# A GELU-gated MLP beside a 2-D spectral filter: head order by tiles, and two chunks transposed by DMA

## Chip, core and metric

The kernel runs on one core of a Trainium2 chip. The metric is the device time of one execution in microseconds (us), as the median of several runs.

## What is computed

```python
x = A_x                                   # (1, 2048, 512) bf16
xn = layernorm(x)                         # over the last axis, eps 1e-5, no scale or shift
X = rfft2(xn) * (w_r + 1j * w_i)          # over both axes; weights (2048, 257)
y = irfft2(X, s=(2048, 512))              # as bf16
g = xn @ w_gate                           # (512, 1792)
u = xn @ w_up
m = (gelu_tanh(g) * u) @ w_down           # (1792, 512)
out = x + y + m
```

## The kernel before

The 2048 rows are 16 tiles of 128 rows. Four tiles are a chunk (`m` or `b`, 0 to 3). All five engines' programs are written out by hand: `_Prog.op` puts an instruction into its engine's list in the order of the calls, and works out from the names of what it reads and writes which semaphores it must wait for. Each engine runs its own list in order.

**Layer norm and transposes.** Per tile VectorE takes statistics (`ln_stat`, L394), aggregates them (`ln_aggr`, L398, L401), GpSimd raises the variance to -1/2 (`rstd`, L402), and VectorE normalizes into `xn`, four slots of `slots` (`ln_norm`, L406). `trans` (L416) transposes 128x128 blocks on TensorE into PSUM, two of the four column blocks (`dcs`) at a time, eight transposes in a call; VectorE (L426) or ScalarE (ACT, L428) copies the result into `xnT`, fp16, 128 columns of `d` on the partitions. In `xnT` a chunk is a range of 512 columns in each of the four `d` blocks.

**The MLP.** For each chunk, 14 blocks `fc` of 128 hidden columns: `gate` (L699, four matmuls over `d`, then Gelu on ACT, L702, into one of three `gl` buffers) and `up` (L714, four matmuls, then on VectorE the product of PSUM and `gl` into `hT`, L720). The down projection of a pair of tiles is done with seven matrix products (`prod`, L805, seven matmuls each) and sums of blocks (`ssum`, L796; `sum_T`, L764), interleaved with the gates and ups of the next chunk.

**The spectral part.** `butter` (L438 to L442) makes sums and differences of the four `d` blocks of `xnT`; it writes into `fold`, a part of `arena`. `unit_D` (L456 to L459) transforms along `d`, one tile a call; `unit_A` (L489) along part of the rows, two tiles a call; its result goes through DRAM, `scr<-slots`, and comes back as `tv<-scr` (`load_tv`), both on SyncE's DMA queue. `unit_Z` and `unit_B` read all of `tv`. `unit_G`, `unit_M`, `unit_B` and `unit_C` apply the filter (with `Wr`, `Wi`, `cm`), then a second trip through DRAM into `arena`, and `unit_E`, `unit_F` and the final sums.

**Order.** The gates and ups are the backbone. After each, `hook` runs the calls that `at(h, ...)` has put at that number; hooks are counted through the whole kernel (28 for chunk 0; 42 for a later chunk, since products count too). So D, A, butterflies, norms and late loads stand at fixed places between gates and ups. `load_late` issues a load on GpSimd's queue (POOL) after the matmuls that precede it. The first loads are issued by SyncE (SP) and ACT at the start, in program order. `take` picks a PSUM bank out of eight from a rough account of when each comes free.

Lines of the head that the change touches, of the kernel before:

```python
for b, eng in ((0, "sp"), (1, "act")):
    load_x(0, 2, b, eng)
    load_x(2, 2, b, eng)
dma("sp", ident[:], c_id.ap(), w=["ident"])
load_w(wg_sb, wgv, "wg", 0, 3, "act")
load_w(wu_sb, wuv, "wu", 0, 3, "sp")
```

Of the kernel before, what the change touches and what calls it, by code (L numbers as in the profile page):

```python
# [18 lines left out]
P = 128  # L19
NJ = 16  # L20
NFC = 14
LN_EPS = 1e-5
# [105 lines left out]
class _Prog:  # L128


    def __init__(self, nc, es):
        self.nc, self.es = nc, es
        self.q = {e: [] for e in ("pe", "act", "dve", "pool", "sp")}
        self.sem = {}
        self.cnt = {}
        self.known = {e: {} for e in self.q}
        self.lastclk = {e: {} for e in self.q}
        self.clk = {}
        self.writer = {}
        self.readers = {}  # L140
        for e in ("pe", "act", "dve", "pool"):
            self.sem[e] = es.enter_context(nc.semaphore("s_" + e))
            self.cnt[e] = 0
        self.dsem = []

    def op(self, eng, fn, r=(), w=(), dma=False, after=(), own=False):
# [4 lines left out]
        for k in w:  # L151
            if k in self.writer:
                deps.append((self.writer[k], False))
            for ev in self.readers.get(k, ()):
                deps.append((ev, False))
        need = {}
        for (st, val), raw in deps:
            if st == eng and not dma and (eng == "pe" or not (raw or own)):
# [22 lines left out]
        else:  # L181
# [3 lines left out]
            for a, b in known.items():  # L185
                if clk.get(a, 0) < b:
                    clk[a] = b
        clk[ev[0]] = ev[1]
# [22 lines left out]
def bass_parallel_sum__spectral_gfnet__glu_gated_geglu__prompt_kernel(  # L211
# [26 lines left out]
    with ExitStack() as es:  # L238
# [24 lines left out]
        arena = sb("arena", [P, 9216], F16)  # L263
        am = arena[:, 0:4096].rearrange("p (j r c) -> p j r c", j=NJ, r=2)
        fold = [arena[:, 4096 + 2048 * i:6144 + 2048 * i].rearrange("p (a c) -> p a c", a=4) for i in range(2)]
        ev1 = arena[:, 8192:9216].rearrange("p (a c) -> p a c", a=2)
# [20 lines left out]
        hz = xnT[:, 3, 256:512].bitcast(F32).rearrange("p (a b c d) -> p a b c d", a=2, b=2, c=16)  # L287
# [35 lines left out]
        pt = [0.0]  # L323
        act_t = [0.0]
        free = [0.0] * 8

        full = [False] * 8

        def take(n, dur, hold=None, need=False, fills=True):

            ok = [i for i in range(9 - n) if not need or all(full[i:i + n])]
            i = min(ok, key=lambda i: max(free[i:i + n]))
            for k in range(i, i + n):
                full[k] = fills
            pt[0] += dur
            if hold is None:
                act_t[0] = max(act_t[0], pt[0] + 0.25) + 0.62
                end = act_t[0]
            else:
                end = pt[0] + hold  # L340
            for k in range(i, i + n):
                free[k] = end
            return i

# [14 lines left out]
        op("dve", lambda e: e.memset(dumm[:], 0.0), w=[("sl", 12)])  # L359
        op("pool", lambda e: e.memset(mhalf[:], -0.5), w=["mhalf"])  # L360
        for b, eng in ((0, "sp"), (1, "act")):
            load_x(0, 2, b, eng)
            load_x(2, 2, b, eng)
        dma("sp", ident[:], c_id.ap(), w=["ident"])
        load_w(wg_sb, wgv, "wg", 0, 3, "act")
        load_w(wu_sb, wuv, "wu", 0, 3, "sp")
        load_w(wg_sb, wgv, "wg", 3, 6, "act")
        op("act", lambda e: e.activation(warm_o[:], mhalf[:, 0:1], ACT.Gelu_apprx_tanh), r=["mhalf"], w=["warm_o"])
        load_w(wu_sb, wuv, "wu", 3, 6, "sp")
        load_x(4, 4, 0, "sp")  # L370
        load_x(4, 4, 1, "sp")
        dma("sp", fd[:], c_fd.ap(), w=["fd"])
        dma("sp", am, c_am.ap().rearrange("p (j r c) -> p j r c", j=NJ, r=2), w=["am"])
        load_w(wg_sb, wgv, "wg", 6, 10, "sp")
        load_w(wu_sb, wuv, "wu", 6, 10, "sp")
        load_x(8, 4, 0, "sp")
        load_x(8, 4, 1, "sp")
        load_w(wg_sb, wgv, "wg", 10, 14, "sp")
        load_w(wu_sb, wuv, "wu", 10, 14, "sp")
# [4 lines left out]
        def warm(n):  # L384
# [5 lines left out]
            op("pe", f, r=[("sl", 12)], w=[("ps", 7)])  # L390
# [5 lines left out]
        def ln_aggr(j0, n):  # L396
            for j in range(j0, j0 + n):
                op("dve", lambda e, j=j: e.bn_aggr(ag[:, j, :], st[:, j, :]), r=[("st", j)], w=[("ag", j)])  # L398
            sl = slice(j0, j0 + n)
            js = range(j0, j0 + n)  # L400
            op("dve", lambda e: e.tensor_scalar(vpe[:, sl], ag[:, sl, 1], LN_EPS, None, ALU.add), r=[("ag", j) for j in js], w=[("vpe", j) for j in js])  # L401
            op("pool", lambda e: e.tensor_tensor(rstd[:, sl], vpe[:, sl], mhalf[:, 0:n], ALU.pow), r=[("vpe", j) for j in js] + ["mhalf"],  # L402
               w=[("rstd", j) for j in js])

        def ln_norm(j):
            op("dve", lambda e: e.tensor_scalar(xn[:, j % 4, :], x_sb[:, j, :], ag[:, j, 0:1], rstd[:, j:j + 1], ALU.subtract, ALU.mult),  # L406
               r=[("x", j, 0), ("x", j, 1), ("ag", j), ("rstd", j)], w=[("sl", 8 + j % 4)])

        def trans(m, dcs, jjs, eng="dve"):
            bk = take(1, 0.45, 1.2, fills=False)  # L410
# [9 lines left out]
            c0 = m * 512 + jjs[0] * P  # L420
            n = len(dcs)
            dst = xnT[:, dcs[0]:dcs[0] + n, c0:c0 + w]
            src = bank_h(bk)[:, 0:n * w].rearrange("p (a c) -> p a c", a=n)
            ks = [("xnT", m, dc, jj) for dc in dcs for jj in jjs]
            if eng == "dve":
                op("dve", lambda e: e.tensor_copy(dst, src), r=[("ps", bk)], w=ks)  # L426
            else:
                op("act", lambda e: e.activation(dst, src, ACT.Copy), r=[("ps", bk)], w=ks)  # L428
# [4 lines left out]
        def butter(m, part):  # L433
            f = fold[m % 2]
            k = ("fold", m % 2)
            sl = slice(m * 512, (m + 1) * 512)
            if part == 0:
                op("dve", lambda e: e.tensor_tensor(ev1, xnT[:, 0:2, sl], xnT[:, 2:4, sl], ALU.add), r=xk(m), w=["ev1"])  # L438
                op("dve", lambda e: e.tensor_tensor(f[:, 2:4, :], xnT[:, 0:2, sl], xnT[:, 2:4, sl], ALU.subtract), r=xk(m), w=[k + (2,), k + (3,)])
            else:  # L440
                op("dve", lambda e: e.tensor_tensor(f[:, 0, :], ev1[:, 0, :], ev1[:, 1, :], ALU.add), r=["ev1"], w=[k + (0,)])
                op("dve", lambda e: e.tensor_tensor(f[:, 1, :], ev1[:, 0, :], ev1[:, 1, :], ALU.subtract), r=["ev1"], w=[k + (1,)])  # L442

# [3 lines left out]
        def unit_D(j):  # L447
# [15 lines left out]
            op("act", lambda e: e.activation(x4[:].rearrange("p (a c r) -> p a c r", a=2, r=4),  # L463
# [15 lines left out]
        def unit_A(h):  # L479
# [17 lines left out]
            op("act", lambda e: e.activation(t4, pair(bk), ACT.Copy, scale=SC_A), r=[("ps", bk), ("ps", bk + 1)], w=tk)  # L497
# [3 lines left out]
            if h % 2:  # L501
                load_tv(h // 2)
# [599 lines left out]
```

## Time and profile before

| What | Value |
|---|---|
| Median of 3 runs (lowest to highest) | 185.04 us (184.81 to 186.04) |
| Profiled execution, its own time | 183.82 us |
| Span of its profile | 182.0 us |
| TensorE (PE) busy | 173.6 us, 95% |
| Weight loads (PEld) | 108.1 us, 59% |
| VectorE (DVE) | 134.7 us, 74% |
| ScalarE (ACT) | 98.2 us, 54% |
| GpSimd (POOL) | 27.3 us, 15% |
| DMA moved | 25.14 MB, 138 GB/s over the span |

The profile is of one execution. It gives the busy time of each engine, the span in 40 slices (4.55 us each), who waited for whom, the chain of work that ended last, and for each DMA issue the time until its data landed. A line such as L699 is a line of the kernel before. TensorE's matmuls are pipelined and their ends are modelled, so the distance from start to start of two groups says more than the duration of one.

### The profile page before, as it was taken

The page shows a single profiled execution, that of the slowest core. Times are in us where ns is not written, and L with a number is a line of the kernel's source. Part 1 is how long each engine was busy: PE and PEld are TensorE (multiplying, and loading weights), DVE is VectorE, ACT ScalarE, POOL GpSimd, SP SyncE. Part 2 cuts the span into 40 slices and gives each one's busy share as a digit, 9 for nine tenths or more (in the row PEclk, how much of TensorE's full clock was granted, in tenths as well). Part 3 has the DMA queues.
Part 4 walks back from the last instruction along what each step waited for, and adds up shares of the span by engine and source line. Part 5 has one row for each costly group of instructions (what it writes and reads, how often), then busy time and mean ns, then how long its engine had stood idle before and what let it go on. Part 6 is the DMA issues. An engine that isn't in the chain of part 4 may idle for free.

```text
span 182.0 us, 3627 instructions
## 1 busy us (share of the span) xinstructions
PE 173.6 (95%) x1413; PEld 108.1 (59%) x1413; DVE 134.7 (74%) x297; ACT 98.2 (54%) x168; POOL 27.3 (15%) x52
## 2 busy tenths in 40 slices
PE   7499998999999999999999999999999999999992
PEld 2285464655555666755466646664577757776881
DVE  1859899898996428359886688465745989788993
ACT  3144537466486633234776557654486667766530
POOL 0200513528444400540100000000000000000000
PEclk9999999999999999999999999999999999999999
DMA  4999997987899872341232224444102211312004
GB/s 128 322 294 368 263 271 250 255 210 165 224 205 296 238 242 61 109 146 39 86 115 79 89 66 119 115 115 119 58 0 60 59 33 32 86 29 59 4 0 115
DMA packets 18785, 25.14 MB, mean 138 GB/s; under 512 B 2128, under 2 KB 15312, under 8 KB 18384
## 3 DMA queue, kind: packets, MB, share of 16 engines
q1 hardware_dynamic: 14848, 16.29, 33.0%
q0 software_dynamic: 2464, 7.38, 14.4%
q10 hardware_dynamic: 1456, 1.25, 2.4%
q8 instruction: 11, 0.18, 0.4%
q14 instruction: 6, 0.05, 0.1%
HBM read 18.61 MB, written 6.29 MB: 137 GB/s over the span
## 4 chain that ended last, share of the span: by engine, by line
PE 76%; DVE 17%; issue 2%; DMA 2%; POOL 1%; ACT 1%; DVEq 0%
PE ps L699 23%; PE ps L714 23%; PE ps L805 18%; DVE small L394 3%; DVE hT L796 3%; PE ps L603 2%; DVE hT L720 2%; PE ps L629 2%; DMA x_sb<-in_A_x_dram 2%; PE ps L667 2%; PE ps L489 2%; PE ps L416 2%; DVE slots L406 1%; POOL rstd L402 1%; PE ps L574 1%
## 5 line engine op out<-in xcount | busy, mean ns | idle before, releaser
L699 PE MATMUL ps<-xnT,wg 128*128 128x512 f16 (+1 forms) x236 | 58.1, 368 | 0.8 <-ACT xnT L428 0.8
L714 PE MATMUL ps<-xnT,wu 128*128 128x512 f16 (+1 forms) x236 | 58.1, 368 | 0.1
L702 ACT ACTIVATE gl<-ps 128x512 bf16<-128x512 f32 (+1 forms) x59 | 34.0, 576 | 41.4 <-PE ps L699 41.0
L720 DVE TENSOR_TENSOR hT<-ps,gl 128x512 bf16<-128x512 f32 (+1 forms) x59 | 38.6, 658 | 18.5 <-PE ps L714 17.8
L699 PEld LDWEIGHTS ps<-xnT,wg 128*128 128x128 bf16 x236 | 22.2, 98 | 19.8 <-issue 1.5
L714 PEld LDWEIGHTS ps<-xnT,wu 128*128 128x128 bf16 x236 | 22.2, 98 | 18.1 <-issue 1.0
L805 PE MATMUL ps<-wd,hT 128*128 128x256 bf16 (+1 forms) x224 | 29.4, 273 | 0.0
L805 PEld LDWEIGHTS ps<-wd,hT 128*128 128x128 bf16 x224 | 21.4, 98 | 7.0 <-DVE hT L796 0.4
L810 ACT ACTIVATE ps<-ps 128x256 f32<-128x256 f32 x32 | 11.8, 369 | 12.2 <-PE ps L805 11.9
L394 DVE BATCH_NORM_STATS2 small<-x_sb 128x6 f32<-128x512 bf16 x16 | 10.8, 682 | 3.1 <-DMA x_sb<-in_A_x_dram 3.0
L463 ACT ACTIVATE slots<-ps 128x512 f16<-128x512 f32 x16 | 9.6, 597 | 5.6 <-PE ps L459 5.5
L585 DVE TENSOR_TENSOR slots<-slots,Wr 128x1024 bf16<-128x1024 f16 x8 | 5.5, 693 | 8.4 <-ACT slots L580 8.2
L611 ACT ACTIVATE slots<-ps 128x1024 bf16<-128x1024 f32 x8 | 8.2, 1024 | 4.4 <-PE ps L603 3.4
L351 POOL DMA_DIRECT2D Wr<-in_A_w_r_dram x16 | 8.0, 498 | 16.8 <-PE ps L714 13.6
L636 ACT ACTIVATE slots<-ps 128x512 bf16<-128x512 f32 x16 | 9.6, 598 | 1.4 <-PE ps L629 1.3
L805 PE MATMUL ps<-xnT,hT 128*128 128x256 f16 x70 | 9.3, 273 | 0.0
L351 POOL DMA_DIRECT2D Wi<-in_A_w_i_dram x16 | 7.9, 497 | 8.1 <-PE ps L714 4.0
L497 ACT ACTIVATE slots<-ps 128x1024 f16<-128x1024 f32 x8 | 7.9, 1022 | 1.8 <-PE ps L489 1.6
L796 DVE TENSOR_TENSOR hT<-hT 128x896 bf16<-128x896 bf16 x14 | 8.5, 620 | 0.2
L673 ACT ACTIVATE slots<-ps 128x1024 bf16<-128x1024 f32 x8 | 8.2, 1022 | 0.7 <-PE ps L667 0.3
L402 POOL TENSOR_TENSOR rstd<-vpe,mhalf 128x4 f32<-128x4 f32 (+1 forms) x5 | 4.6, 920 | 24.0 <-DVE vpe L401 24.0
L580 ACT ACTIVATE slots<-ps 128x1024 f16<-128x1024 f32 x8 | 8.2, 1020 | 0.0
(93 smaller groups left out, 207.2 us busy)
## 6 DMA issues: line engine op xcount, KB each, us to landing
Wr<-in_A_w_r_dram POOLq DMA_DIRECT2D x16, 128.5 KB, 4.6
Wi<-in_A_w_i_dram POOLq DMA_DIRECT2D x16, 128.5 KB, 3.7
scr<-slots SPq DMA_DIRECT2D x16, 128.0 KB, 4.1
tv<-scr SPq DMA_DIRECT2D x8, 256.0 KB, 4.1
scr<-slots SPq DMA_DIRECT2D x8, 256.0 KB, 2.3
arena<-scr SPq DMA_DIRECT2D x8, 256.0 KB, 3.5
x_sb<-in_A_x_dram SPq DMA_DIRECT2D x6, 256.0 KB, 12.0
out_dram<-x_sb SPq DMA_DIRECT2D x10, 128.0 KB, 2.4
```

The lines of the kernel that those rows point to most:

```text
L351: op("pool", lambda e: e.dma_start(dst, src), w=keys, dma=True, after=[("pe", pr.cnt["pe"])])
L394: op("dve", lambda e: e.bn_stats(st[:, j, :], x_sb[:, j, :]), r=[("x", j, 0), ("x", j, 1)], w=[("st", j)])
L463: op("act", lambda e: e.activation(x4[:].rearrange("p (a c r) -> p a c r", a=2, r=4), bank(bk).rearrange("p (a r c) -> p a c r", a=2, r=4) ...
L580: op("act", lambda e: e.activation(xc[s2], pair(bk), ACT.Copy, scale=SC_B), r=[("ps", bk), ("ps", bk + 1)], w=ck)
L636: op("act", lambda e: e.activation(z[:], bank(bk).rearrange("p (a c) -> p a c", a=4), ACT.Copy, scale=SC_E), r=[("ps", bk)], w=[zk])
L699: ins = e.matmul(bank(bg)[:, 0:n], wg_sb[:, dc, fc * P:(fc + 1) * P], xnT[:, dc, c0:c0 + n], start=(dc == 0), stop=(dc == 3))
L702: op("act", lambda e: e.activation(gl[k % 3][:, 0:n], bank(bg)[:, 0:n], ACT.Gelu_apprx_tanh), r=[("ps", bg)], w=[("gl", k % 3)])
L714: ins = e.matmul(bank(bu)[:, 0:n], wu_sb[:, dc, fc * P:(fc + 1) * P], xnT[:, dc, c0:c0 + n], start=(dc == 0), stop=(dc == 3))
L720: op("dve", lambda e: e.tensor_tensor(hT[b % 2][:, fc, h0:h0 + n], bank(bu)[:, 0:n], gl[k % 3][:, 0:n], ALU.mult), r=[("ps", bu), ("gl", k ...
L796: op("dve", lambda e: e.tensor_tensor(Ss[i][0], a, c, o), r=ak + ck + (Ss[2][1] if i == 3 else []), w=Ss[i][1])
L805: ins = e.matmul(o, L[:, fc, :], R[fc], start=(start and fc == 0), stop=(fc == 6), skip_group_check=True)
L810: op("act", lambda e: e.activation(half(y, k), half(x, i), ACT.Copy), w=bkey(x, y), own=True)
```

## The change

- *Loads.* The first two tiles of x are loaded one by one (half on SyncE, half on ACT); all weights are loaded from SyncE's queue; x of chunk 1 comes in two parts between the weights; `fd` and `am` come after it; x of chunks 2 and 3 comes last.
- *Head.* Statistics, norm, transposes and copies of tiles 0 and 1 are done tile by tile. The gates of blocks 0 to 2 are then computed for tile 0 and after that for tile 1 (`gates_by_tile`). Six blocks (`NH`) instead of three are first computed for tiles 0 and 1 only, and for tiles 2 and 3 after them.
- *Chunks 2 and 3.* Each is transposed by one DMA from `slots` into `xnT` on SyncE's queue (`trans_dma`), in a layout where the four `d` blocks of a tile stand side by side; `xd` gives the view of a chunk in either layout, and `gate`, `up` and `butter` read through it. Chunks 0 and 1 stay on TensorE (`MT`).
- *Butterfly.* The first sums go to `fold` itself and one extra row (`evx`); the last addition is in place.
- *Hooks.* Norms, transposes, butterflies, D, A, `load_tv`, `sum_T` and the late loads stand at other hooks.
- *Banks.* `_Prog` keeps an estimated time for each engine and event (`c=` gives an instruction's), and `take` picks a bank by when its last user is expected to finish. The wait of the second `up` product (`wait=True`) is dropped; `gl` is addressed by block and tile.

```diff
+NH = 6
+MT = 2
+TVH = (5, 5, 5, 4)
...
+        def xd(m):
+            if m < MT:
+                return xnT[:, m, :].rearrange("p (d j t) -> p d j t", d=4, j=4)
+            return xnT[:, m, :].rearrange("p (j d t) -> p d j t", d=4, j=4)
...
-        for b, eng in ((0, "sp"), (1, "act")):
-            load_x(0, 2, b, eng)
-            load_x(2, 2, b, eng)
-        dma("sp", ident[:], c_id.ap(), w=["ident"])
-        load_w(wg_sb, wgv, "wg", 0, 3, "act")
+        for j in range(2):
+            for b, eng in ((0, "sp"), (1, "act")):
+                load_x(j, 1, b, eng)
+        dma("act", ident[:], c_id.ap(), w=["ident"])
+        load_w(wg_sb, wgv, "wg", 0, 3, "sp")
+        load_x(2, 2, 0, "sp")
+        load_x(2, 2, 1, "sp")
         load_w(wu_sb, wuv, "wu", 0, 3, "sp")
-        load_w(wg_sb, wgv, "wg", 3, 6, "act")
+        load_w(wg_sb, wgv, "wg", 3, 6, "sp")
...
         load_w(wu_sb, wuv, "wu", 3, 6, "sp")
-        load_x(4, 4, 0, "sp")
-        load_x(4, 4, 1, "sp")
+        load_x(4, 2, 0, "sp")
+        load_x(4, 2, 1, "sp")
+        load_w(wg_sb, wgv, "wg", 6, 10, "sp")
+        load_w(wu_sb, wuv, "wu", 6, 10, "sp")
+        load_x(6, 2, 0, "sp")
+        load_x(6, 2, 1, "sp")
         dma("sp", fd[:], c_fd.ap(), w=["fd"])
         dma("sp", am, c_am.ap().rearrange("p (j r c) -> p j r c", j=NJ, r=2), w=["am"])
-        load_w(wg_sb, wgv, "wg", 6, 10, "sp")
-        load_w(wu_sb, wuv, "wu", 6, 10, "sp")
+        load_w(wg_sb, wgv, "wg", 10, 14, "sp")
+        load_w(wu_sb, wuv, "wu", 10, 14, "sp")
         load_x(8, 4, 0, "sp")
         load_x(8, 4, 1, "sp")
-        load_w(wg_sb, wgv, "wg", 10, 14, "sp")
-        load_w(wu_sb, wuv, "wu", 10, 14, "sp")
         load_x(12, 4, 0, "sp")
         load_x(12, 4, 1, "sp")
...
+        def trans_dma(m):
+            op("sp", lambda e: e.dma_start_transpose(xnT[:, m, :].rearrange("p (a c) -> p a c", a=16), slots[:, 8:12, :].rearrange("p a c -> p (a c)")),
+               r=[("sl", 8 + jj) for jj in range(4)], w=[("xnT", m, dc, jj) for dc in range(4) for jj in range(4)], dma=True)
...
             else:
-                op("dve", lambda e: e.tensor_tensor(f[:, 0, :], ev1[:, 0, :], ev1[:, 1, :], ALU.add), r=["ev1"], w=[k + (0,)])
-                op("dve", lambda e: e.tensor_tensor(f[:, 1, :], ev1[:, 0, :], ev1[:, 1, :], ALU.subtract), r=["ev1"], w=[k + (1,)])
+                op("dve", c=0.34, fn=lambda e: e.tensor_tensor(f[:, 1, :], f[:, 0, :], evx, ALU.subtract), r=["evx", k + (0,)], w=[k + (1,)])
+                op("dve", c=0.45, fn=lambda e: e.tensor_tensor(f[:, 0, :], f[:, 0, :], evx, ALU.add), r=["evx"], w=[k + (0,)], own=True)
...
-        for u0, h0 in ((0, 20), (12, 28), (4, 36), (8, 57)):
+        for u0, h0 in ((0, 24), (12, 33), (4, 56), (8, 64)):
...
-        for m in range(1, 4):
-            a = 9 * (m - 1) + 3
-            t = a + 9 + (m == 1)
...
-        for j in range(NJ):
-            h = (9, 11, 13, 15, 18, 20, 22, 23, 26, 28, 30, 32, 35, 36, 37, 38)[j]
-            at(h, (unit_D, j))
-            if j % 4 == 3:
-                at(h + 2, (unit_A, j // 2 - 1), (unit_A, j // 2))
-        at(29, (sum_T, 1))
-        at(31, (sum_T, 2))
-        at(34, (sum_T, 3))
-        at(35, (sum_T, 4))
+        for m, (sh, nh, t, te, f, dh, ah) in enumerate((
+                ((), (), 0, (), (12, 13), (17, 18, 19, 20), (22, 22)),
+                ((2, 3, 8, 10), (13, 14), 17, ("dve", "dve"), (20, 21), (24, 25, 26, 27), (29, 29)),
+                ((22, 23, 24, 25), (27, 28), 28, ("dve", "dve"), (34, 35), (38, 39, 40, 41), (43, 43)),
+                ((32, 33, 36, 37), (39, 40), 40, ("act", "act"), (46, 47), (50, 51, 52, 53), (55, 55)))):
+            for i, h in enumerate(sh):
+                at(h, (ln_stat, 4 * m + i))
+                at(nh[i // 2], (ln_norm, 4 * m + i))
+            if m:
+                at(sh[3], (ln_aggr, 4 * m, 4))
+                if m < MT:
+                    at(t, (trans, m, (0, 1), (0, 1, 2, 3), te[0]))
+                    at(t + 1, (trans, m, (2, 3), (0, 1, 2, 3), te[1]))
+                else:
+                    at(t, (trans_dma, m))
+            for part, h in enumerate(f):
+                at(h, (butter, m, part))
+            for i, h in enumerate(dh):
+                at(h, (unit_D, 4 * m + i))
+            for i, h in enumerate(ah):
+                at(h, (unit_A, 2 * m + i))
+            at(ah[1] + TVH[m], (load_tv, m))
+        for i, h in ((1, 30), (2, 32), (3, 37), (4, 42)):
+            at(h, (sum_T, i))
...
-        warm(14)
+        warm(12)
         ln_stat(0)
+        ln_aggr(0, 1)
         ln_stat(1)
-        ln_aggr(0, 2)
-        ln_stat(2)
+        ln_aggr(1, 1)
         ln_norm(0)
         ln_norm(1)
+        for jj in range(2):
+            trans(0, (0, 1), (jj,), "dve")
+            trans(0, (2, 3), (jj,), "act")
+        ln_stat(2)
         ln_stat(3)
...
+        gates_by_tile((0, 1, 2))
+        up(0, 0, (0, 1))
         ln_norm(2)
         ln_norm(3)
...
+        up(0, 1, (0, 1))
+        up(0, 2, (0, 1))
+        gate(0, 3, (0, 1))
+        gate(0, 4, (0, 1))
         trans(0, (0, 1), (2, 3), "dve")
         trans(0, (2, 3), (2, 3), "act")
+        gate(0, 5, (0, 1))
...
-                jjs = (2, 3) if b == 0 and fc < 3 else (0, 1, 2, 3)
+                jjs = (2, 3) if b == 0 and fc < NH else (0, 1, 2, 3)
+                if b == 0 and fc == 3:
+                    for f2 in range(3, NH):
+                        up(0, f2, (0, 1))
```

## The prediction

> **What bounds the kernel now.** I read the slices of the span first, then who waited for whom on TensorE, the chain that ended last, the groups by shape, the DMA issues and the queue of SyncE in order of time.
>
> ```profile
> PE   7499998999999999999999999999999999999992
> DVE  1859899898996428359886688465745989788993
> PEclk9999999999999999999999999999999999999999
> ```
>
> TensorE is full from the third slice to the last, at the full granted clock, so time can only come from its first 31 us, from its list of work, or from the tail. VectorE is nearly full in slices 3 to 12.
>
> ```profile
> PE ps L416 <- DVE slots L406: 2.3, 2, 1.6
> PE ps L699 <- ACT xnT L428: 0.8, 1, 0.8
> PE ps L456 <- DVE arena L442: 0.6, 1, 0.6
> ```
>
> These are all of TensorE's waits between 7 and 36 us (total, times, longest): 1.6 before the first transpose and 0.8 before the first gate, then 0.7 before chunk 1's transpose at 23.1 (norms late) and 0.6 before chunk 1's first D at 30.8 (butterfly late). After 30.8 starts follow each other without a gap until about 170.
>
> ```profile
> 0.74 3.33 DMA x_sb<-in_A_x_dram
> 4.09 1.29 DVE small L394 x2
> 5.38 0.23 DVE small L398 x2
> 5.63 0.18 DVE vpe L401
> 5.89 0.74 POOL rstd L402
> 6.65 0.75 DVE slots L406 x2
> 7.53 0.62 PE ps L416 x8
> 8.17 0.61 ACT xnT L428
> 8.91 0.60 PE ps L699 x4
> ```
>
> This is the start of the chain (start, us, what): two tiles together, step after step, until the first gate at 8.91. The steady prices come from the same view: eight transposes 0.45, a half-width gate or up 0.44, a full one 0.86, a product 0.765, an A pair 0.98, a D 0.34.
>
> **The change, part by part.**
>
> *Head.* x tiles come one by one and each is normalized and transposed alone. A first half tile is 64 KB. The trace has no such load: 64 KB stores land in 2.0 us, the quickest 128 KB load took 2.8. I take 2.6 (bounds 2.0, and 3.3 as now), so tile 0 is there at 3.3. Statistics 0.68, aggregate 0.15, epsilon 0.18 and steps between: 4.4. The same for tile 1: 5.3. GpSimd's first rstd (0.74) is done by 5.2, the second by 6.1. Norm 0 runs at 5.3, norm 1 at 6.15 to 6.5, and behind it on VectorE the copy of tile 0's transposes (0.42 for twice the columns, so some 0.28). First gate at 6.9 instead of 8.91: **-2.0** (bounds -2.5, -1.2). The two warm-up matmuls removed lie before that; ACT's queue now carries the identity (4.2 us to land now; needed at 5.7). Cover that must hold: the first gate weights are third on SyncE's queue. Ahead of them and with them are 0.69 MB, with tiles 2 and 3 0.95 MB; the slices' rates (128, then 322 GB/s) move that by 5.7, so they land about 6.2, 0.7 before use. Later weights are covered: six blocks on half the columns push block 6 from 14.7 or so (block 3 full now) to 18.7, and its weights are within the first 3.4 MB, there by 14. Chunk 2's x, now behind all weights, is within 6.5 MB of SyncE's loads plus 1 to 1.8 MB of w_down, 27 to 29 us; its statistics come at 31.
>
> *Two waits.* The 0.7 and 0.6 go, since chunk 1's norms and butterfly now sit three or more hooks ahead of use on a less loaded VectorE. I count a new 0.3 where tiles 2 and 3 are copied before their first gate: **-1.0** (bounds -1.3, 0).
>
> *Chunks 2 and 3.* Four groups of eight transposes leave TensorE's full stretch: 4 x 0.45 = **-1.8**, no bound needed. Four copies (0.60 apart) leave VectorE, where TensorE hides them.
>
> *Half blocks.* Three more blocks split: 6 x (2 x 0.44 - 0.86) = **+0.15**. The tile-major layout reads 128-column runs in matmuls and butterflies; shapes stay, and I price this at nothing (no row shows such runs; 1% on the 56 gates and ups of chunks 2 and 3 would be 0.5, on either side).
>
> *Other edits at nothing.* Banks by finish times: TensorE waits on no bank now, and a bad choice would show as a new wait on ACT or VectorE. The butterfly's add in place waits for the subtraction before it, 0.1 or so on VectorE, which TensorE hides except at D. Wr, Wi and cm loads on GpSimd's queue move to later hooks; the last Wi load, at hook 71, has eight hooks (6.5 us) before unit_G reads it, and such loads land in 3.7 to 4.6. The tv loads keep their place in SyncE's order, but for the transposes between them.
>
> Sum so far: -4.65. Adding up the work in the new order gives the same: first D of chunk 2 on TensorE near 47.6, A of chunk 3 at 65.3, Z at 76.5 instead of 81.2.
>
> *The new waits.* Chunks 2 and 3 now wait for one 512 KB DMA each on SyncE, and the butterfly that needs it sits on VectorE, in order: behind it are the products hT of gate and up, behind those the three gl buffers and PSUM banks, and so TensorE.
>
> ```profile
> scr<-slots SPq DMA_DIRECT2D x16, 128.0 KB, 4.1
> tv<-scr SPq DMA_DIRECT2D x8, 256.0 KB, 4.1
> wg<-in_B_w_gate_dram SPq DMA_DIRECT2D x2, 512.0 KB, 11.4
> wd<-in_B_w_down_dram POOLq DMA_DIRECT2D x2, 512.0 KB, 9.8
> ```
>
> No transposing DMA is in this trace (columns: count, size, us to landing). Low end 3.3, the quickest tv load of half the bytes; high end 11.4, the same bytes in a full queue. I take 5.1: the tv load, same queue and same stretch, plus 256 KB more at some 250 GB/s (1.0). It is nearer to tv, because the queues of 35 to 60 us are not the head's.
> The Trainium skill speaks against the change: "VectorE: DVE Perf Modes", The three transpose paths and Rules for kernel authors, lists 390 ns for a 128x128 transpose on TensorE, 1309 by DMA, and advises TensorE where PSUM will do. Sixteen in a row by that figure would be 21 us a chunk (an estimate), and the kernel some 25 us slower. Against it stands 56 ns a transpose in the row above. "DMA: Bandwidth & Descriptors", Latency and other measured facts, gives 261 GB/s for a strided DMA transpose, by which the data alone is 2.0 us (an estimate) and the sum mine.
>
> ```profile
> 29.91 2.66 SPq L347 DMA_DIRECT2D scr<-slots  x4
> 35.95 1.37 SPq L347 DMA_DIRECT2D tv<-scr  x2
> ```
>
> Chunk 2: SyncE reaches the transpose only past the stores and tv loads of chunk 0. Now A starts at 28.2, the second tv load issues at 36.8, 8.6 later. A will start at 30.4, so the transpose issues at 39.6; the norms are done at 38.9. VectorE, by its order (statistics, products, sum_T 1 and 2 at 1.0, norms 1.5 for four, all from the rows), reaches the butterfly at 45.0. Room 5.4: **0**, and 1 us for each us beyond. Chunk 3: norms end at 54.0. From there two sums (0.54), sum_T 4 (1.05) and two products (0.6) come first, and D for chunk 3 is on TensorE at 59.9 with 1.9 of butterfly ahead. Room 4.0: **+1.1**. How long the transpose holds SyncE I don't know: 0.6 like other issues, or all 5; behind it are only scr stores and tv loads of chunks 1 and 2, whose reader is Z, 25 us on.
>
> Chunk 3's spectral path loses its cover. Its A starts at 57.8 now and Z reads tv at 81.2: 23.4 us. In the new order only the A (0.98), six products, six gates or ups and the small G work lie between: 11.0 us. The way through is eviction (first one ends 1.7 after A starts), four stores at 0.66, landing 2.4 to 4.8, tv landing 3.3 to 4.5: 10 to 13.1 us (now all batches take 13.1 or more, with fuller DMA queues). I take 11.5: **+0.5** (bounds 0, 2.1).
>
> Total -4.65 + 1.6 = -3.05. The profiled execution took 183.82 for a span of 182.0, 1.2 under the median 185.04; so 180.8 for one like it, and **182.0** on the median's scale.
>
> **Rivals.**
> 1. *The transposes are hidden.* They land in 4 us or less and the tv path takes 11: 185.04 - 4.65 = 180.4. For it: 3.3 to 3.8 for tv loads at 59 to 67 us. Against: DMA engines 0.8 to 1.0 busy from 30 to 60.
> 2. *The gain turns into waits.* Landing near 6.8: stalls 1.4 + 2.8 + 0.5 cancel 4.65: 185.1. For it: tv loads issued at 45 us took 6.5 to 8.0. Against: those ran beside a full run of Wr and Wi loads, which now leave the stretch of chunk 3's transpose.
> 3. *Slower.* The transposing DMA itself is slow, in place at both butterflies. The price is 2L - 9.4 for a landing L over 5.4; L = 10 gives 10.6, and 185.04 - 4.65 + 0.5 + 10.6 = 191.5. It decides from L = 6.8 on, and is over 1% slower from 7.7. For it: 9.8 and 11.4 for 512 KB. Against: these were queued behind megabytes.
> 4. *The head does less*: x lands at 4.1 as before, first gate at 7.7: 182.8. On the forecast's side of no change.
>
> **How the numbers follow.** A measurement of this kernel tells about 1% from no change: under 183.2 is faster, over 186.9 slower. Forecast with rival 4 (180.8 to 183.2) 0.48, rival 1 0.20, rival 2 0.16, rival 3 0.16. So faster 0.68, same 0.16, slower 0.16. The forecast's own range is 180.2 to 183.6; 179.5 to 186.7 leaves out rival 3 and little below.
>
> **What would show it.** First gate near 6.9, no wait over 0.4 on TensorE from 12 to 45; no transposes of chunks 2 and 3 there; a DMA xnT<-slots twice, about 5 us to landing; VectorE's butterfly (arena<-xnT) for chunk 3 waiting about 1 us for it and TensorE's D behind; Z near 78, waiting for tv 0.5 or so. Wrong: a landing over 7 us, a first gate after 8, or new gaps between 12 and 36 us because weights or x come late.

## The result, and the profile after

The changed kernel took 190.44 us (median of 4 runs, 189.56 to 191.24), the kernel before beside it 185.54; the ratio is 1.0285, 95% interval 1.0218 to 1.0351. The forecast was 182.0 (179.5 to 186.7). The profiled execution took 189.97 for a span of 188.0; before, 183.82 for 182.0. Here and below a median is over all executions of a kernel, and a ratio leaves out those more than 1.5% above its fastest. Lines below are of the changed kernel: D is L482, the butterfly L464 to L469, Z L539, A L515, gate L740, up L754, the DMA transpose L452.

The slices of the span (4.7 us each):

```profile
PE   7699999999499999969999999999999999999992
DVE  3748978777698755337597678637555789887993
PEclk9999999999969999996999999999999999999999
```

TensorE now has two holes, in slices 11 and 18, and in the granted clock the slice behind each has a dip. Who waited for whom on TensorE (total, times, longest):

```profile
PE ps L482 <- DVE arena L469: 2.6, 1, 2.6
PE ps L539 <- DMA tv<-scr: 2.1, 1, 2.1
PE ps L410 <- DVE slots L377: 1.2, 1, 1.2
PE ps L754 <- DMA wu<-in_B_w_up_dram: 0.9, 1, 0.9
PE ps L438 <- DVE slots L428: 0.7, 2, 0.4
PE ps L740 <- ACT xnT L449: 0.3, 1, 0.3
PE ps L598 <- DVE hT L759: 0.3, 1, 0.3
```

The waits of before at chunk 1's transpose and D are gone. New are D of chunk 2 (2.6), Z (2.1) and the first up (0.9). The chain that ended last shows what stands behind them (start, us, what), here its stretch around chunk 2's transpose:

```profile
37.54 2.36 DMA tv<-scr
39.89 8.73 DMA xnT<-slots
...
51.39 0.23 PE ps L482
...
53.79 1.71 PE ps L740 x4
```

The transpose is issued at 39.89 (forecast 39.6) but lands 8.73 later, at 48.6, where the forecast had 5.1. VectorE stood 2.1 for it, TensorE 2.6 (VectorE's waits for both transposes: total, times, longest):

```profile
DVE arena L464 <- DMA xnT<-slots: 2.7, 2, 2.1
```

The gate at 53.79 then takes 1.71, twice its 0.86, since the clock is down. The windows of 1 us show it (window, PE, PEld, DVE, ACT, POOL busy, granted clock, DMA share, GB/s):

```profile
52.00:53.00 1.00, 1.00 (x5) 0.30 (x4) 1.00 (x2) 0.53 (x1) 0.00 (x0) 0.61 0.90 273
53.00:54.00 1.00, 1.00 (x6) 0.62 (x5) 0.97 (x7) 0.17 (x1) 0.30 (x1) 0.50 0.01 0
54.00:55.00 1.00, 1.00 (x4) 0.44 (x3) 1.00 (x2) 0.43 (x1) 1.00 (x1) 0.50 0.74 262
55.00:56.00 1.00, 1.00 (x7) 0.58 (x6) 1.00 (x3) 0.47 (x1) 1.00 (x2) 0.68 0.07 16
```

Four windows give up 0.39 + 0.50 + 0.50 + 0.32 = 1.7 us of full clock. Chunk 3's transpose, issued at 57.6, lands in 5.4; VectorE stands 0.5 for it, TensorE not at all. The second hole is the trip of chunk 3's A through DRAM, in the same chain:

```profile
75.02 3.97 DMA scr<-slots
...
79.05 5.78 DMA tv<-scr
...
84.96 0.22 PE ps L539 x4
...
86.33 1.54 PE ps L754 x4
```

A starts at 71.33 and tv's last load lands at 84.83, 13.5 later (forecast 11.5); Z waits 2.1, and another dip of the clock follows. Meanwhile GpSimd's queue, in order of time:

```profile
42.15 0.49 POOL L369 DMA_DIRECT2D Wi<-in_A_w_i_dram  x1 [1.46 <-PE ps L740]
43.01 0.49 POOL L369 DMA_DIRECT2D Wi<-in_A_w_i_dram  x1 [0.37 <-PE ps L754]
43.88 0.57 POOL L369 DMA_DIRECT2D cm<-c_cm  x1 [0.38 <-PE ps L740]
44.74 0.50 POOL L369 DMA_DIRECT2D Wr<-in_A_w_r_dram  x1 [0.28 <-PE ps L754]
```

A load goes out nearly every 0.9 us from 38 to 48.7, and again from 73.5 to 84. Of the four groups of `load_late`, the first two (hooks 24 and 33) stand beside chunk 2's transpose, the other two (hooks 56 and 64) beside tv's trip. The DMA issues of the changed kernel (count, KB, us to landing):

```profile
scr<-slots SPq DMA_DIRECT2D x16, 128.0 KB, 3.2
tv<-scr SPq DMA_DIRECT2D x8, 256.0 KB, 4.0
xnT<-slots SPq DMA_TRANSPOSE x2, 7.1
```

### The profile page after: what moved, and what is told of

Its sections match the earlier page's. It is cut to its first block, busy times and chain, and to the rows that moved or that the text cites. A ratio compares the mean times of both kernels' runs of the same rounds, so it can differ in the third digit from the quotient of the medians.

```text
span 188.0 us, 3640 instructions
## 1 busy us (share of the span) xinstructions
PE 176.0 (94%) x1415; PEld 108.7 (58%) x1415; DVE 133.3 (71%) x298; ACT 99.0 (53%) x172; POOL 28.8 (15%) x53
## 4 chain that ended last, share of the span: by engine, by line
PE 68%; DMA 16%; DVE 9%; issue 2%; SPq 2%; ACT 1%; DVEq 0%
PE ps L754 21%; PE ps L740 21%; PE ps L840 15%; DMA xnT<-slots 5%; DMA tv<-scr 4%; DMA scr<-slots 4%; DMA wu<-in_B_w_up_dram 3%; DVE hT L831 3%; PE ps L627 2%; SPq L365 2%; PE ps L653 2%; PE ps L691 2%; PE ps L515 1%; DVE hT L759 1%; PE ps L598 1%
## 5 line engine op out<-in xcount | busy, mean ns | idle before, releaser
L754 PE MATMUL ps<-xnT,wu 128*128 128x512 f16 (+1 forms) x248 | 59.1, 365 | 0.9 <-DMA wu<-in_B_w_up_dram 0.9
L740 PE MATMUL ps<-xnT,wg 128*128 128x512 f16 (+1 forms) x236 | 58.4, 372 | 0.3 <-ACT xnT L449 0.3
L744 ACT ACTIVATE gl<-ps 128x512 bf16<-128x512 f32 (+1 forms) x59 | 33.4, 567 | 45.0 <-PE ps L740 43.4
L754 PEld LDWEIGHTS ps<-xnT,wu 128*128 128x128 bf16 x248 | 23.6, 99 | 19.5 <-issue 2.1
L740 PEld LDWEIGHTS ps<-xnT,wg 128*128 128x128 bf16 x236 | 22.4, 99 | 20.7 <-issue 2.1
L424 POOL TENSOR_TENSOR rstd<-vpe,mhalf 128x4 f32<-128x4 f32 (+2 forms) x6 | 5.8, 968 | 13.2 <-DVE vpe L423 13.1
```

The source lines that it names most:

```text
L740: ins = e.matmul(bank(bg)[:, 0:n], wg_sb[:, dc, fc * P:(fc + 1) * P], x4[:, dc], start=(dc == 0), stop=(dc == 3))
L744: op("act", c=0.12 + 0.00075 * n, fn=lambda e: e.activation(g, bank(bg)[:, 0:n], ACT.Gelu_apprx_tanh), r=[("ps", bg)], w=gk)
L754: ins = e.matmul(bank(bu)[:, 0:n], wu_sb[:, dc, fc * P:(fc + 1) * P], x4[:, dc], start=(dc == 0), stop=(dc == 3))
```

## The experiments

Theory A: the transposes and tv's trip land late because GpSimd's loads are in flight beside them (the expectations say: they share the DMA engines). Theory B: the chain (norms, transpose, butterfly, D, A, stores, tv, Z) is too long by its own steps, by VectorE's order or by the DMA transpose as such. Theory C: the clock after the idle is the cost.

### Undoing the DMA transposes

```diff
-MT = 2
+MT = 4      # e1_mt4: all chunks on TensorE;  e2_mt3: MT = 3, chunk 2 on TensorE
```

> The changed kernel with chunks 2 and 3 transposed on TensorE again (MT = 4), all else as changed. Theory A (the DMA transpose lands late: 8.7 us for chunk 2, so VectorE's butterfly comes late, TensorE idles 2.6 us before chunk 2's first D and then runs at half clock for some 3.4 us): the 2.6 shrinks to 1.5 or less, since VectorE reached the butterfly 2.1 us before the landing but now has two copies more (1.2 us), and TensorE does 1.8 us more; if the idle falls under what drops the clock, 1.7 comes back as well. Time about 187 to 189, and the wait at Z and the half clock after it stay. Theory B (VectorE's order is late by itself): idle before D of chunk 2 stays at 2.5 or more, time 190 to 192.

> The changed kernel with only chunk 3 transposed by DMA, chunk 2 on TensorE (MT = 3). Theory A (only chunk 2's landing hurt, chunk 3's 5.4 us was hidden): 0.9 us better than the kernel with both chunks on TensorE, and 2 to 4 us better than the changed kernel: 186 to 188. Theory B (both DMA transposes cost): no better than both on TensorE.

All on TensorE: 192.88 us, ratio 1.046 (1.0389 to 1.053), slower still. TensorE's waits there:

```profile
PE ps L438 <- DVE slots L428: 4.7, 3, 3.4
PE ps L539 <- DMA tv<-scr: 3.0, 1, 3.0
```

D's wait is gone, but the transposes stand in the changed order at the hook of the last two norms, and now TensorE itself waits 3.4 for chunk 3's, longer than either theory expected. Z waits as before. Chunk 2 alone on TensorE: 189.74, ratio 1.0263 (1.0173 to 1.0352), D of chunk 3 waiting 0.8 and Z 2.8. So taking the DMA away doesn't bring the time back, which speaks for B or for the loads.

### Keeping the clock

```diff
+            if m == 2:
+                at(dh[0], (fill, 11))     # 11 matmuls of 512 columns, results unused
...
+        at(b0, (fill, 9))
         at(b0, (unit_Z,) ...
```

> The changed kernel with 11 matmuls of 512 columns into an unused bank right before chunk 2's first D and 9 right before Z; they use ready operands and lie inside TensorE's two waits (2.6 and 2.1 us). Theory C (an idle of 2 us drops the granted clock to 0.5 for some 3.4 us, 1.7 us lost each time): the clock stays at 1.00 through 45 to 92 us, and the time falls by 3 to 3.5 us to about 187, though not one wait is shorter. Rival (the clock falls for the load of the stretch, or the lost time is a wait counted otherwise): no gain, or up to 0.5 us slower.

190.19, ratio 1.0316 (1.0225 to 1.0407): no gain. The clock stayed at 1, but chunk 2's transpose landed in 10.1 this time, so D waited 1.65 behind the fill, and chunk 3's D a new 1.4. Neither of these two shorter waits was followed by a dip. The run alone doesn't decide on C, since the landing moved too; the starts in the table further down do.

### The DMA operations by themselves

A kernel that computes nothing of the reference and only moves tiles about.

> No computation of the reference, only x copied through; on SyncE's queue, one after the other and each waited for: a DMA transpose of 512 KB between tiles in SBUF, a plain copy of 512 KB, a plain copy of 512 KB in runs of 256 bytes, transposes of 256 KB and 128 KB, two of 256 KB back to back, and last one of 512 KB while GpSimd issues 16 loads of Wr and Wi. Theory A1 (the transpose is slow by itself): 512 KB alone takes 5 us or more to land, at least 2 us more than the plain copy, and the loads add little. Theory A2 (it was the other DMA traffic): 3.5 to 4.5 alone, 7 or more beside the loads. If the cost is in the 256-byte runs, the plain copy in such runs takes as long as the transpose.

A 512 KB transpose alone landed in 4.4, one of 256 KB in 3.0, of 128 KB in 2.4; a plain copy of the 512 KB in 2.9, in runs of 256 bytes in 4.1. Two 256 KB transposes back to back landed in 3.2 and 3.1. The 512 KB transpose with 16 loads of Wr and Wi queued around it landed in 8.8, near the changed kernel's 8.73. Each is one value of one execution. This is the first sign for A.

### Moving GpSimd's loads

```diff
-        for u0, h0 in ((0, 24), (12, 33), (4, 56), (8, 64)):
+        for u0, h0 in ((0, 46), (12, 46), (4, 67), (8, 67)):    # e6_loads
+        for u0, h0 in ((0, 20), (12, 28), (4, 36), (8, 57)):    # e11_oldloads: hooks of the kernel before
```

> GpSimd's loads of Wr, Wi and cm leave the stretches in which chunk 2's and chunk 3's transposes and tv's loads are under way: the first two groups go to hooks 46 to 54, behind chunk 3's transpose, the last two to hooks 67 to 75, behind Z. No other engine's order changes. Theory A (shared DMA engines): the 8.7 us of chunk 2's transpose are queueing with the loads; alone it takes 4.4, beside 16 such loads 8.8. Then chunk 2's landing falls to 4.5 to 5.5, VectorE and D wait nothing, tv's second load falls from 5.8 to about 4, Z waits under 0.5, the clock stays at 1, and the 2.6 + 2.1 of waits and the 3.4 lost to the clock go: 183 to 185 us. Theory B (the chain norms, transpose, butterfly, D, A, stores, tv is too long by its own steps): landing stays above 7, waits stay at 2 to 3 us, the time at 189 to 191.

187.46, ratio 1.0147 (1.0066 to 1.0228), some 3 us of the loss back. No other engine's list changed. The landings of the two transposes, then TensorE's waits:

```profile
DMA to landing us min/median/max: 4.3/4.4/4.4
```

```profile
PE ps L539 <- DMA tv<-scr: 2.1, 1, 2.1
PE ps L482 <- DVE arena L469: 0.4, 1, 0.4
```

Both transposes land as they do alone and D's wait falls to 0.4. As VectorE no longer stands for chunk 2's landing, this 0.4 is VectorE's own order: so much of B is true. Z's wait stayed, as this stretch of the chain shows:

```profile
71.53 6.05 DMA scr<-slots
...
78.26 3.72 DMA tv<-scr
```

The loads at hooks 46 to 54 went out from 59.9 to 69 and kept the DMA engines near 1.0 until 76 us. The last four stores of A's result landed in 5.7 to 6.7 beside them, so that tv's loads went out only at 77.6. That is A as well, at a place where the expectation missed it.

> The changed kernel with GpSimd's loads at the hooks of the kernel before (20, 28, 36 and 57): the one part of the change that moved them is undone. Theory A: the second and third group (hooks 28 to 45) still run beside chunk 2's transpose, which lands in 8 to 10 with a wait of 2 to 4 at D, and only the last group (57 to 65) runs near tv's loads, whose second landing falls from 5.8 to about 4.5, so that Z waits under 1: 187.5 to 190. Theory B: the same as the changed kernel within 1 us, Z waiting 2.

202.16, ratio 1.0775 (1.0622 to 1.0928), far outside what either theory expected. With the loads at their old hooks and the changed order of everything else, TensorE's wait and the landings:

```profile
PE ps L482 <- DVE arena L469: 13.9, 2, 13.2
```

```profile
DMA to landing us min/median/max: 6.5/12.3/18.0
```

Chunk 2's transpose lands in 18.0, chunk 3's in 6.5. So in this order the loads stood worse at their old hooks than where the change put them, and the landing isn't proportional to the loads beside it: nine are issued during the flight in both kernels, for 8.7 and for 18.0.

### Z later, and TensorE's transposes behind the norms

```diff
-        b0 = 67
+        b0 = 70                                        # e4_b70
...
-  ... (27, 28), 28, ...      -  ... (39, 40), 40, ...   # MT = 4, e7_mt4late and,
+  ... (27, 28), 31, ...      +  ... (39, 40), 43, ...   # with e6_loads' hooks, e8_both
```

> Z and all that hangs on its hook (B, C, E, F) three hooks later: about 2.6 us more of gate, up and down work on TensorE ahead of Z. Theory A and B alike: Z's wait of 2.1 and the half clock behind it (1.7) go, chunk 2's stall stays (2.6 and 1.7). If TensorE's order sets the end, 186.5 to 188. If the chain from Z through C, E and F to the last stores sets the end instead, the gain is eaten by waits at E or at the end of the kernel and the time stays at 189 to 191.

194.04; its executions scatter from 189.68 to 195.84, so no ratio is given. Z no longer waited, but in the profiled execution chunk 2's transpose, with the same loads around it, landed in 11.5 and D waited 5.4. That landing is not a fixed price: 8.7, 10.1 and 11.5 in one profiled execution each of three kernels whose lists are the same up to its issue.

> All chunks transposed on TensorE, as in the run that did only this, but the transposes of chunks 2 and 3 stand three hooks behind their norms (hooks 31 and 43 in place of 28 and 40), as chunk 1's do. The theory that the earlier run was slow for its hooks and not for TensorE's transposes: its waits of 4.3 before the transposes and the half clock behind them go, 1.8 us of transposes stay, Z still waits 2 to 3 and loses 1.7 of clock: 186.5 to 188.5. If the norms are late by more than three hooks, it waits again and stays at 190 or more.

> The transposes on TensorE three hooks behind the norms and GpSimd's loads moved behind chunk 3's transposes and behind Z. Against the run with the loads moved alone it tells what the two DMA transposes are worth once nothing disturbs them: four evictions fewer and 1.8 us less on TensorE. If theory A holds, this is 1 to 2 us slower than that run: 184.5 to 186.5. If the DMA transposes still cost waits there, this one is the faster of the two.

188.48 (ratio 1.0163, 1.0063 to 1.0262) and 188.95 (1.0221, 1.0128 to 1.0315). By the ratios, three hooks of distance take some 5 us off the run with TensorE's transposes (1.046 to 1.0163): most of its loss was in its hooks. Z still waited 1.8 and 2.1.

### Loads in the gaps

```diff
+        for u0, h0 in ((0, 34), (12, 34), (4, 45), (8, 67)):    # e9_spread, and wu(0:3) ahead of tiles 2, 3
+                                                                # e10_spread_mt4: MT = 4 at hooks 31, 43
+        for u0, h0 in ((0, 34), (12, 46), (4, 67), (8, 67)):    # e12_clean, and the second G two hooks later
+                                                                # e13_clean_mt4: the same with MT = 4 at 31, 43
+        load_w(wu_sb, wuv, "wu", 0, 3, "act")                   # e14_clean_wuact: e12_clean and this
```

> The changed kernel with GpSimd's loads spread over the stretches where no transpose and no tv load is under way: the first two groups two to a hook from hook 34 (45.5 to 56 us), the third one to a hook from 45, the fourth from 67, behind Z; and the first up weights ahead of tiles 2 and 3 in SP's order at the head. Theory A (landings are lengthened by the loads they share the DMA engines with): both transposes land in 4.3 to 5, tv's second load in about 4 in place of 6.7, Z waits under 0.5, the wait for Wi (0.7) goes, the wait for the up weights at the head (0.8) goes or passes to tiles 2 and 3. From the run with the loads moved (186.3 profiled): less 2.1, 0.7, 0.5 and some 0.5 of clock: 182.5 to 184.5. Theory B (the chain to Z is too long by its own steps): Z waits 2 us as it did in every run of this order, 186 to 187.5.

> The same loads, with chunks 2 and 3 transposed on TensorE three hooks behind their norms in place of the two DMA transposes. TensorE gets 1.8 us of transposes more and VectorE and ScalarE four evictions; nothing stands on SP in front of the stores. By the size of the step in the prediction, 1.8 us slower than the same loads with the DMA transposes; if the DMA transposes still cost a wait, 0 to 1; with Z waiting for tv as before, 187 to 188.5.

A miss in the first: 189.94, ratio 1.0225 (1.0163 to 1.0287). Chunk 2's transpose landed in 4.4 and Z didn't wait. But GpSimd's queue stood for chunk 3's rstd until 53.9, and the eight Wi loads and two of cm behind it went out from there to 59, around chunk 3's transpose (issued at 56.1), which landed in 9.0; D of chunk 3 waited 4.5. With TensorE's transposes, where no such landing exists, the same loads gave 185.47, ratio 0.9987 (0.9957 to 1.0017). The first up's wait passed to tiles 2 and 3 (1.0 and 1.3 at their transposes).

> The changed kernel with GpSimd's loads in the three stretches that no transpose and no tv load needs: the first group at hooks 34 to 42 (45.5 to 55 us), the second at 46 to 54 (60.5 to 70), the last two behind Z, two to a hook; the second G two hooks later. The head is the changed kernel's. Theory A (the loss is landings lengthened by loads beside them): both transposes land in 4.3 to 5, tv's last load in about 4.5, D waits 0.4 twice at most, Z under 0.5, Wi nothing, the clock stays at 1: from the changed kernel's 190 less 2.2, 1.8, 3.4 and little more: 182 to 184. Theory B (VectorE's order and the steps of the chain set the end): some wait of 2 us shows again at D of chunk 3 or at Z, and 186 to 188.

> The same loads with chunks 2 and 3 transposed on TensorE, three hooks behind their norms. It prices the two DMA transposes with nothing beside them: the prediction's step says they take 1.8 us off TensorE, so this one is 1.5 to 2.5 us slower than the run with the same loads, 184 to 186.5. If it is as fast or faster, the step was worth nothing even undisturbed, since TensorE waits elsewhere for what VectorE and SP have to do.

> As the run with the clean loads, and the first up weights issued by ScalarE's queue behind its two loads of tile 0 and 1 and ident, in place of SP's fifth step. If the wait of 0.9 at the first up comes from the weights being issued at 4.08, it goes and 0.8 to 1 us with it: 181 to 183. If it comes from the bandwidth that the first loads share, the wait moves to the gate weights or to tiles 2 and 3 and nothing is gained.

184.55, ratio 0.9973 (0.9939 to 1.0006): the loss against before is gone by moving the loads (and the second G, two hooks later). D of chunk 3 still waited 1.45. With TensorE's transposes the time was 185.18 (0.9991, 0.9953 to 1.0028), only 0.6 more, 0.3 by the ratios. The up weights on ScalarE's queue gave 184.9 (0.9994, 0.9961 to 1.0028): the wait for them left, and the gate weights were waited for instead (1.0). An earlier issue moved the wait and did not remove it; that the first loads lack bandwidth fits this, but no run shows it.

### The last collision, and what the DMA transposes are worth

In the run of 184.55, too, GpSimd's queue stood for chunk 3's rstd, and five loads behind it went out at 53.7 to 55.7, just ahead of chunk 3's transpose at 55.85, which landed in 5.9. So, with the hooks of that run, the first group goes ahead of the rstd, two to a hook:

```diff
-                        at(h0 + 4 * k + 2 * c + ri, (load_late, ...
+                        at(h0 + (4 * k + 2 * c + ri) // (1 if u0 else 2), (load_late, ...
-            at(h0 + 8, (load_late, cm[:, hs], ...
+            at(h0 + (8 if u0 else 12), (load_late, cm[:, hs], ...
```

> The run with the clean loads had one collision left: GpSimd's queue stands at 49 us for chunk 3's rstd, and the four Wi loads and cm behind it went out at 53.7 to 55.7, just ahead of chunk 3's transpose at 55.85, which landed in 5.9. Here the first group's loads go out two to a hook, all ahead of that rstd, and its cm with the second group. Theory A: chunk 3's transpose lands in 4.4, VectorE's wait of 2.6 falls to 1.1, D's wait of 1.45 to about 0: 184.6 less 1.3, 183 to 184. If D keeps waiting, VectorE's order is late there by itself and the time stays at 184.5.

183.43, ratio 0.9882 (0.9837 to 0.9927): 0.7 to 1.6% faster than the kernel before. Slices, TensorE's waits and the landings of the two transposes:

```profile
PE   7799999999999999999999999999999999999992
PEclk9999999999999999999999999999999999999999
```

```profile
PE ps L410 <- DVE slots L377: 1.2, 1, 1.2
PE ps L438 <- DVE slots L428: 0.6, 2, 0.4
PE ps L754 <- DMA wu<-in_B_w_up_dram: 0.5, 1, 0.5
PE ps L482 <- DVE arena L469: 0.4, 1, 0.4
```

```profile
DMA to landing us min/median/max: 4.3/4.4/4.4
```

No hole and no dip are left. VectorE no longer stands for chunk 2's landing (the 0.4 at L482 is chunk 2's D, waiting for VectorE's own order), and D of chunk 3 doesn't wait. Only GpSimd's list and the second G (with its M), two hooks later, tell this kernel from the changed one, and 7 us lie between them. Six of these are there at Z already, ahead of that G, so it is the place of the loads that makes them: the cause is shown.

> As the run before it, with chunk 3's four D and its A one hook later (hooks 51 to 54 and 56). If D still waits there, this takes up to 0.9 of the wait away; tv's last load goes out 0.9 later, and Z still has 0.5 to 1 in hand: 183 to 184 where D waited, the same time where it did not.

With D of chunk 3 one hook later 183.33 (0.9887, 0.9825 to 0.9949): the same, as D of chunk 3 no longer waited.

> The loads of the run with the first group ahead of chunk 3's rstd (183.4), with chunks 2 and 3 transposed on TensorE three hooks behind their norms. It prices the two DMA transposes with no load beside them. By the step of the prediction 1.8 us slower, 185 to 185.5; with no gain left in them, 183.2 to 184.

185.1, ratio 0.9988 (0.9952 to 1.0023): with nothing of GpSimd's beside them the two DMA transposes are worth 185.1 - 183.43 = 1.7 us (2.0 by the two ratios, which were taken on different chips), near the 1.8 of the prediction's step.

## Why the prediction was wrong

Starts on TensorE, as forecast and in the profiles (us):

| | forecast | changed | loads moved (183.43) | before |
|---|---|---|---|---|
| first gate | 6.9 | 6.86 | 6.88 | 8.91 |
| first D of chunk 2 | 47.6 | 51.39 | 48.93 | |
| A of chunk 3 | 65.3 | 71.33 | 67.52 | 57.83 |
| Z | 76.5 to 78 | 84.96 | 78.98 | 81.20 |
| end | | 188.0 | 180.6 | 182.0 |

Between the two middle columns the 7.4 us fall as follows: 2.5 up to D of chunk 2 (mostly its wait), 1.35 up to A (the clock after it), 2.2 up to Z (its wait), 1.4 behind Z (the clock again).

1. *Head: right in size, one cover wrong.* First gate at 6.86 for 6.9. The prediction checked the cover of the gate weights, and not of the up weights, which are sixth on SyncE's queue. They land at 9.25, and 0.9 was lost (0.5 to 1.3 in the other runs with this head):

```profile
4.08 5.17 DMA wu<-in_B_w_up_dram
```

2. *Two waits and the four groups of transposes: right.* The waits at chunk 1 are gone, the 0.3 at tiles 2 and 3 is 0.34, and the transposes are worth 1.7 when nothing disturbs them.

3. *The landing of chunk 2's transpose, priced at 5.1: the step that failed.* It measured 8.73; without GpSimd's loads beside it, in the same order, 4.4, so 5.1 was even high for a quiet flight. The price came from tv loads of "the same queue and same stretch", by their median of 4.1, and the working did not ask what each of them flew beside. The row with the same company was in the trace of before, and the prediction quoted it under rival 2: the pair of tv loads issued at 44.8 took 6.5 to 8.0, in the middle of the Wr and Wi loads.

```profile
DMA to landing us min/median/max: 6.5/7.2/8.0
```

```profile
42.59 1.55 POOL L351 DMA_DIRECT2D Wi<-in_A_w_i_dram  x3
44.13 0.62 POOL L351 DMA_DIRECT2D cm<-c_cm  x1
44.74 1.47 POOL L351 DMA_DIRECT2D Wr<-in_A_w_r_dram  x3
```

With the prediction's 1.0 for the larger size, that row gives 7.5 to 9.0 (an estimate). Rival 2 set the row aside because the loads leave the stretch of chunk 3's transpose. They don't leave chunk 2's: from 34 to 49 us GpSimd issued 13 of them before and 14 after. "Other edits at nothing" shares in this, since it asked of the moved loads only whether the last one comes in time for unit_G. But the move by itself was not the loss: with the old hooks the changed order took 202.16.

The waits worked out from the landing were off too. VectorE reached chunk 2's butterfly at 46.5, not 45.0, so that 8.73 cost VectorE 2.1 and not 3.3, and D came another 0.4 late by VectorE's order. For chunk 3 the forecast added 1.1 to TensorE; VectorE did stand 0.5 and, with the loads moved, 0.9, but TensorE waited for nothing.

4. *tv's trip: the same error.* Forecast 11.5, measured 13.5 with the last two groups beside it; Z waited 2.1 where 0.5 was forecast. With these loads behind Z the trip took 11 and Z waited for nothing.

5. *Missing altogether: the clock.* The prediction priced a wait at its own length. Each of the two idles drew some 3.4 us at half clock behind it, which cost 1.35 and 1.4 between the starts of the table. The run with the fill agrees: there D of chunk 2 to A took 19.65 with a wait of 1.4 in it, 18.25 without, against 19.94; and Z to the end 101.8 against 103.0. So C is real, but second: without the idles there is no dip. The Trainium skill, "TensorE: Matmul & The Clock Gate" (Part 1: The HAM clock gate), describes such a clock: half speed after an idle window of about 3.4 us, full speed again after about 3.4 us of work. The traces agree with the half speed, and the full clock came back 2.9 to 4.6 us after the work resumed; but here idles of 1.8 to 2.8 us were enough five times.

6. *Rivals.* Rival 3 had the place and the outcome (a slow landing, 191.5 for 10 us), but gave it 0.16 and blamed the transposing DMA itself; its price 2L - 9.4 charged both chunks, and only chunk 2 was late. The Trainium skill's 1309 ns for one DMA transpose, in "VectorE: DVE Perf Modes" (The three transpose paths), taken sixteen times would have made a chunk cost some 21 us (an estimate). Alone a chunk took 4.4, so the measurement decides against that reading; the prediction's "some 25 us slower" for it would have been 28 by its own price 2L - 9.4 and the rest of its sum.

7. *What stays open.* Even with the loads moved, Z comes at 78.98 where the forecast's sum, with the 0.9 of waits left there, has 77.4, and from Z to the end it is 101.6 for 100.8 before. These 1.6 and 0.8 are why 183.43 and not 181 came out; no run looked for them. Nor is it settled why nine loads made 8.7 once and 18.0 once, or what in the DMA engines makes a landing beside loads long: the runs show that the loads do it, not how.

## What to carry to other kernels

When a transfer is put on the path that sets the end, list what every queue issues between its issue and its landing in the new order, and price it from a row with the same company; an edit that only moves loads is not free. When freeing one landing, look at where the loads go next: here one placement hit the stores of tv's trip, and two hit chunk 3's transpose, because the queue stood for rstd and let the loads out late. A wait of 2 us or more on TensorE should be priced with a range that includes a dip of the clock behind it.

## What the runs showed of the hardware

- A DMA transpose of 512 KB from SBUF to SBUF took 4.4 alone, 8.7 to 11.5 with the loads of the changed kernel beside it, and 18.0 with them at their old hooks.
- It holds SyncE's queue: 1.3 and 1.9 in the run of 183.43. For chunk 2 it held 4.23 in the changed kernel and 6.39 in the run of 202 us, and the stores behind it in the list went out only then, at 44.18 and 48.16.
- Each of these transposes goes in some 2080 packets of under 512 bytes: with none, one and two of them (otherwise the changed order) the profile counts 2192, 4272 and 6352.
- An idle of TensorE was often followed by a granted clock of 0.50 (3.4 us of it after each idle of the changed kernel), but length alone doesn't tell. Of the twelve waits of 1.8 us or more in these profiles nine drew such a dip (the shortest 1.82 long), and three did not: 2.07 and 2.27 before Z with the loads moved and with the loads at their old hooks, and 2.97 before Z with all transposes on TensorE.
